# A searched instruction order and u on another DMA queue in an RWKV-6 and squared-ReLU kernel

## The chip, the cores and the metric

The kernel runs on one core of one Trainium2 chip. The metric is the device time of one execution in microseconds (us); lower is better. The engines of the core are TensorE (PE, with PEld for its weight loads), VectorE (DVE), ScalarE (ACT), GpSimd (POOL) and SyncE (SP). Each runs its own instructions strictly in the order in which the program gives them. SP only issues DMAs here.

## The reference

Two stages. The first is an RWKV-6 attention with B=4, H=8, S=768 tokens and head size D=48; r, k, v, w have the shape [B, H, S, D] and u has [H, D]:

```python
for t in range(S):
    cur = einsum('bhd,bhe->bhde', u[None] * kt, vt)
    y[:, :, t] = einsum('bhd,bhde->bhe', rt, state + cur)
    state = wt[:, :, :, None] * state + einsum('bhd,bhe->bhde', kt, vt)
```

Its output is laid out as x, [3072, 384], and goes through an MLP with w_in [384, 2048], w_out [2048, 384] and scalars s and b. The result is [3072, 384] in float32:

```python
h = x @ w_in
r = np.maximum(h, 0.0)
g = s * (r * r) + b
out = g @ w_out
```

## The kernel before

**The work.** The 3072 tokens are 24 chunks n of 128 tokens. Within a chunk the recurrence is done with matrix products, and a small state goes from a chunk to the next one of its batch. Two chunks make a token tile T of 256 tokens, and the MLP runs tile by tile (T = 0 to 11). Chunks 0 to 3 are "packed": they are loaded in pairs of 384 KB (load2, L316), the others by four loads of 192 KB (load, L308).

**The steps of a chunk**, by the names that the order uses: `load n.0` to `n.3` bring w, r, k and v. `ln` (ACT, L331 and L339) takes the log of w, `cum` (PE, L390 to L414) sums it over the chunk, `exp` and `exn` (ACT, L438, L456) and `inc` (DVE, L446) turn the sums into decay factors, `mul` (DVE, L465 and L472) multiplies r and k by them into the tile prd. `rkp` and `rku` (POOL, L344, L350) form r*k and then times u, `cd` (DVE, L367) sums that over a head, `yd` (POOL, L373) multiplies v by it. The transposed r and k (tile RK) come for n < 9 from TensorE (`tr`, L521) and a copy `tev` (L535 on ACT, L537 on DVE), and from n = 9 on from a DMA transpose on SP's queue, which is also called `tev` (dtrans, L558). `mt` (PE, L588 and L600; one step for two chunks) forms the products of k and r, `msk` (DVE, L612) masks them, `ymm`, `ydm`, `ymi` (PE) form y, `dmm` (PE), `sup` (DVE) and `st` (POOL) bring the state forward, `yev` (L741) writes y as x. x is transposed on TensorE for n < 20 (`xtr`, L787, with the copy `xev`) and by a DMA transpose from n = 20 on (dxtr, L568). `vb` casts v to bf16 on the engine that its label names.

**The steps of a tile.** `g1` T.0 to T.7 are 6 matmuls each (L841), `relu` follows on ACT (L854), `sq` squares on ACT (L864) or DVE (L866), `g2` T.0 to T.7 are 4 matmuls each (L884), `oev` scales and adds the bias on DVE (L895), and `store` writes on SP's queue (L913, L917). `li`, `lo` load the weights in pieces and `ci`, `co` cast them; `csred`, `csadd`, `cssplit`, `csspread`, `csevac` form the bias b * sum(w_out). `load_u` (L983) loads u as one row, `u_mm` (L987) spreads it over the partitions with two matmuls, and `u_ev` copies it out; rku needs it.

**What sets the order.** ORDER (from L42) is a list of all steps, written out as text. The program walks it, and each step issues its instructions on its engine, so the list fixes every engine's order, and SP's queue as well: loads, DMA transposes and stores go into one queue in list order. `+n` puts n independent warm-up matmuls on TensorE (L1263). A suffix `@A`, `@D` or `@P` writes ACT, DVE or POOL into the step's entry. A step acts on it only where its function asks for it, as `move` (packed yev, tev, xev, u_ev), `square`, `cast`, `csred` and `csadd` do:

```python
def relu(T, i):
    rh = mlp.tile([128, FPQ, TOK], BF16, name="rh", tag="rh", bufs=4)
    nc.scalar.activation(out=rh, in_=hs[T, i], func=AF.Relu)
...
    if pl.ops["sq", T, i]["eng"] == "ACT":
        nc.scalar.activation(out=g, in_=rh, func=AF.Square)
    else:
        nc.vector.tensor_tensor(out=g, in0=rh, in1=rh, op=ALU.mult)
```

The unpacked yev is written with nc.vector in the same way as relu with nc.scalar. Tiles live in rings of buffers (5 for w, 8 for r and k, 6 for v, 6 PSUM buffers for products, 2 for u_ps, o_ps and the warm-ups), and a step that takes a buffer waits until the last user of the one before is done.

Of the kernel before, what the change touches and what calls it, by code (L numbers as in the profile page):

```python
# [18 lines left out]
U_AT = 3.5  # L19
# [23 lines left out]
load0.0 load_u load0.1 load0.2 ln0 +6 u_mm cum0.0 cum1.0 cum1.1 exp0.0 exp0.1 load2.0 li0 load2.1  # L43
exp1.0 u_ev@A l20 l21 load0.3 rkp1 rku1 load2.2 mul0.0 mul0.1 +4 tr0 exp1.1 mul1.0 ln2 +4 cum2.0
rkp0 mul1.1 tr1 tev0@D exp2.0 cum3.0 cd1 tev1@A vb0@A exp2.1 vb1@A +3 mt0 rku0 li1 cum3.1 ci0@A rkp3
exp3.0 rkp2 mul2.0 load2.3 msk1.0 exp3.1 ci1@A li3 li2 msk0.0 lo0 msk1.1 +3 ymm0.0 msk0.1 cd0 dmm0
ymm0.1 mul2.1 sup0 yd0 yd1 vb3@A vb2@A rku3 st0 mul3.0 l23 sup1 load4.0 tr2 ymi0 ydm0 lo1 rku2
mul3.1 tr3 tev2@A yev0@A xtr0 yev1@D xtr1 xev0@D ci3@P cd3 tev3@A xev1@A ci2@A mt2 cd2 g10.0 msk2.0
yd2 g10.1 l22 yd3 relu0.0 co0@A li4 msk3.0 msk2.1 co1@P g10.2 ymm2.0 lo2 ln4 lo3 load5.0 dmm2 msk3.1
sup2 ymm2.1 st2 g10.3 csred0@D ydm2 cum4.0 sq0.0@A relu0.2 ci4@P relu0.1 ymi2 yev2@D g10.4 sq0.2@A  # L50
relu0.3 xtr2 sup3 csred1@D exp4.0 sq0.1@D small2 g10.5 co2@D g10.6 xev2@A lo4 yev3@A xtr3 csadd1@D
sq0.3@A relu0.4 csred2@D relu0.6 load4.1 g10.7 relu0.5 g20.4 xev3@A sq0.4@A co3@D ln5 csadd2@D
sq0.5@A g20.0 cum4.1 g20.5 g20.1 g11.0 g11.1 load4.3 load7.0 csred3@D relu0.7 co4@D sq0.6@A csadd3@D
cum5.0 g11.2 sq0.7@A load5.1 load4.2 l24 csred4@D small cum5.1 g20.6 load5.2 relu1.1 relu1.0 g20.2
relu1.2 exp4.1 csadd4@D cssplit sq1.0@A load5.3 g20.3 g11.3 mul4 g11.4 vb5@P exp5.0 g11.5 exp5.1
sq1.1@A sq1.2@A vb4@A relu1.3 relu1.4 rkp4 rkp5 g20.7 csspread g11.6 tr4 load8.0 load6.0 csevac mul5
rku4 l25 oev0.1 relu1.5 tev4@A tr5 tev5@D oev0.0 rku5 dmm4 load7.3 load6.1 sup4 load6.2 relu1.6
g11.7 g21.0 mt4 msk4.0 msk5.0 load6.3 load7.1 sq1.3@A sq1.4@A sq1.5@A sq1.6@A relu1.7 st1 g21.1
g21.4 g21.5 dmm5 ln6 load9.0 msk4.1 cd4 yd4 ymm4 cum6.1 msk5.1 cum6.0 ln7 cd5 sup5 ln8 st4 exp6.0
cum7.0 g21.2 sq1.7@A exp6.1 vb6@A g21.6 cum7.1 yev4 exp7.0 vb7@P st5 ymm5 g21.3 xtr4 exp7.1 cum8.0  # L60
yd5 l26 ln9 mul6 tr6 yev5 xev4@D st3 load7.2 exp8.0 xtr5 dmm6 mul7 cum9.0 g21.7 tr7 tev6@A inc8
xev5@A sup6 load10.0 load11.0 l28 dmm7 load8.3 load8.1 load11.3 load9.1 l27 sup7 exp9.0 g12.0 g12.1
tev7@A relu2.0 inc9 oev1.0 rkp6 mt6 rku6 rkp7 relu2.1 store0.0 load8.2 msk6.0 sq2.1@A g12.2 ln10
sq2.0@A g12.3 st7 cd6 exn9 exn8 relu2.3 relu2.2 sq2.3@A load9.2 store0.1 msk6.1 oev1.1 g12.4 msk7.0
sq2.2@A rku7 st6 yd6 msk7.1 g22.0 ymm6 g22.4 load9.3 g12.5 cd7 yev6 relu2.4 ymm7 g12.6 yd7 vb8@P
xtr6 cum10.0 g12.7 rkp9 l29 mul8 ln11 relu2.5 exp10.0 rkp8 relu2.6 xev6@D load10.1 yev7 g22.1 inc10
xtr7 sq2.6@A xev7@D cum11.0 dmm8 l210 g22.5 tr8 load10.3 g13.0 sup8 mul9 load11.1 tev8@D inc11
sq2.4@A load10.2 relu2.7 exn10 load11.2 g13.1 sq2.5@A tev9 rku9 load14.1 g22.2 g13.2 g22.6 vb11@P
relu3.0 vb10@A sq2.7@A exp11.0 g22.3 load13.0 rku8 load12.0 g13.3 cd9 relu3.2 exn11 vb9@A sq3.2@A
relu3.1 dmm9 sq3.1@A sq3.0@D g22.7 g13.4 load12.1 g13.5 mul10 oev2.0 sup9 relu3.3 cd8 sq3.3@A mul11  # L70
l211 rkp10 yd8 rkp11 st8 yd9 mt8 relu3.5 relu3.4 oev2.1 g23.4 msk9.0 g23.5 g23.0 load13.1 msk8.0
msk9.1 sq3.5@A dmm10 g13.6 ln12 msk8.1 ymm9 ln13 sq3.4@A rku10 relu3.6 ymm8 cum13.0 yev9 sup10
cum12.0 g23.1 exp12.0 load13.2 g13.7 yev8 xtr9 tev11 sq3.6@A exp13.0 inc13 xtr8 g23.6 dmm11 g23.2
xev8@A st9 rku11 rkp13 xev9@A relu3.7 g14.0 cd10 tev10 inc12 cd11 sup11 sq3.7@A relu4.0 load12.3
store1.0 g14.1 mt10 relu4.1 msk10.0 msk10.1 msk11.0 load14.0 l213 l212 load12.2 store1.1 load15.1
load13.3 load15.0 store2.0 load18.0 rku13 st10 yd10 st11 g14.2 g14.3 g14.4 g23.7 msk11.1 exn12 g14.5
yd11 ymm11 ymm10 exn13 sq4.0@A relu4.2 relu4.3 ln14 relu4.4 load14.2 load16.0 oev3.1 mul12 yev11
yev10 sq4.3@A g23.3 vb12@A sq4.1@A sq4.2@D g14.6 cum14.0 xtr10 relu4.5 mul13 load15.2 g24.0 xev10@D
tev12 tev13 sq4.4@D xtr11 exp14.0 relu4.6 g24.1 g14.7 dmm12 xev11@A g15.0 inc14 l214 sq4.6@A sq4.5@A
oev3.0 load17.0 g15.1 g15.2 ln15 rkp12 exn14 relu4.7 sq4.7@A cum15.0 relu5.1 g24.4 g24.2 inc15  # L80
relu5.0 sq5.1@D sup12 exp15.0 vb13@A g15.3 g24.5 exn15 cd13 store2.1 dmm13 mul14 relu5.3 sup13 rku12
rkp15 cd12 relu5.2 l215 rkp14 ln16 sq5.0@A g24.6 rku14 rku15 g24.3 g15.4 relu5.4 sq5.3@A g15.5
relu5.5 mul15 oev4.0 mt12 msk12.0 g24.7 msk12.1 load14.3 load15.3 tev15 load16.1 st12 msk13.0 oev4.1
ln17 sq5.2@A g15.6 yd12 cum16.0 load16.2 cum17.0 msk13.1 sq5.4@A yd13 exp16.0 g25.4 g25.5 vb15@A
g25.0 vb14@P inc16 l216 st13 rkp16 relu5.6 ln18 ymm13 sq5.6@A ymm12 inc17 cd14 g25.1 tev14 g15.7
yev12 yev13 xtr12 sq5.5@A exp17.0 xev12@A relu5.7 exn16 exn17 load17.1 dmm15 load16.3 load19.0 xtr13
dmm14 g25.6 cum18.0 xev13@D sq5.7@A sup15 g25.2 store3.1 store3.0 g16.0 g25.7 sup14 mt14 inc18 mul16
msk14.0 relu6.0 exp18.0 l218 st15 yd14 vb16@P sq6.0@A g25.3 cd15 yd15 g16.1 g16.2 g16.3 load17.2
msk15.0 relu6.1 relu6.2 relu6.3 msk14.1 msk15.1 g16.4 oev5.1 g16.5 rkp17 ymm14 sq6.1@A relu6.4 ln19
mul17 oev5.0 l217 load18.3 st14 tev16 load18.1 relu6.5 yev14 tev17 load17.3 ymm15 g26.4 g16.6  # L90
load18.2 store4.1 store4.0 rku17 g16.7 rku16 sq6.3@A sq6.2@A sq6.5@A load20.0 yev15 sq6.4@D load21.1
xtr14 cum19.0 dmm16 g26.0 load21.0 load19.1 xtr15 g26.1 xev14@D relu6.6 g26.2 xev15@D sup16 relu6.7
sq6.7@A exp19.0 g17.0 g17.1 cd17 relu7.0 load20.1 inc19 cd16 sq7.0@A vb17@P yd16 vb18@A load19.2
mt16 msk16.0 msk16.1 g26.5 sq6.6@A g17.2 msk17.0 st16 relu7.1 g26.6 dmm17 sup17 msk17.1 g17.3 ymm16
g26.7 yev16 oev6.1 rkp18 relu7.2 relu7.3 ymm17 g17.4 load20.2 yd17 st17 g26.3 xtr16 oev6.0 sq7.1@A
exn18 xev16@D yev17 g17.5 g17.6 load21.2 load19.3 ln20 exn19 rku18 mul18 g27.4 xtr17 sq7.2@A relu7.4
g27.0 g17.7 sq7.4@A relu7.5 relu7.6 ln21 sq7.5@D store5.0 xev17@D cum20.0 sq7.3@A rkp19 relu7.7 cd18
g18.0 mul19 l219 g18.1 vb19@P rku19 exp20.0 sq7.6@A load22.0 inc20 sq7.7@D cum21.0 g18.2 g27.5 g27.1
g27.6 exn20 relu8.0 tev18 g18.3 relu8.1 relu8.2 exp21.0 g27.2 dmm19 store5.1 sq8.2@A g27.3 g27.7
mul20 inc21 exn21 dmm18 relu8.3 sq8.0@D tev19 sq8.1@A cd19 mul21 g18.4 load23.0 g18.5 yd19 rkp20  # L100
g18.6 sup18 tev21 sup19 oev7.1 oev7.0 relu8.4 ln22 yd18 rkp21 mt18 sq8.3@A relu8.5 g28.0 st18
msk19.0 supn21 msk18.0 msk19.1 tev20 msk18.1 load20.3 rku20 g28.4 g18.7 load22.1 store6.1 relu8.6
sq8.5@A ln23 cum22.0 g28.1 rku21 inc22 ymm18 cd20 cum23.0 ymm19 sq8.4@A relu8.7 exp23.0 g28.5 supn20
yev18 yev19 inc23 load22.2 xtr18 g28.2 xtr19 exp22.0 mt20 load23.1 msk20.0 load23.2 cd21 msk20.1
msk21.0 g28.6 yd20 exn22 sq8.7@A xev18@A xev19@A mul22 exn23 supn22 sq8.6@A store6.0 g19.0 load21.3
msk21.1 vb20@A g19.1 rkp22 g28.3 g19.2 relu9.1 ymm20 g19.3 g28.7 yd21 vb21@P relu9.0 yev20 oev8.0
relu9.2 sq9.1@D g19.4 g19.5 sq9.0@A relu9.4 relu9.5 relu9.3 store7.1 sq9.4@A g19.6 g19.7 sq9.3@A
g29.4 tev22 rku22 sq9.2@A mul23 oev8.1 g29.0 ymm21 xev20 sq9.5@D relu9.6 tev23 relu9.7 sq9.7@A rkp23
load22.3 sq9.6@A yev21 cd22 st19 xev21 yd22 vb22@P load23.3 g29.1 g29.2 g29.5 g29.6 mt22 g29.7 g29.3
msk22.0 msk23.0 g110.0 msk22.1 g110.1 vb23@P ymm22 relu10.0 rku23 msk23.1 oev9.1 relu10.1 yev22  # L110
store8.1 store7.0 g110.2 cd23 supn23 yd23 sq10.0@D g110.3 g110.4 g110.5 ymm23 oev9.0 store8.0
relu10.2 sq10.2@D yev23 store9.1 relu10.5 sq10.1@A xev22 relu10.3 sq10.3@A relu10.4 sq10.5@A xev23
# [56 lines left out]
def kernel(  # L169
# [812 lines left out]
    def load_u():  # L982
        nc.sync.dma_start(out=u_row, in_=u.rearrange("h d -> (h d)").unsqueeze(0))  # L983
# [320 lines left out]
```

## Time and profile before

| | |
|---|---|
| median of 7 runs | 182.85 us (181.62 to 183.75) |
| profiled execution | 183.69 us |
| its span | 181.9 us |
| granted TensorE clock | 0.998 |
| DMA | 34.53 MB, mean 190 GB/s, 110065 of 115722 packets under 512 bytes |
| chain that ended last | PE 67%, ACT 8%, DMA 8%, SPq 6%, POOL 4%, DVE 4% |
| largest lines in it | o_ps L884 28%, h_ps L841 26% |

The span is cut into slices or windows; for each engine its busy time is given, for the DMA the mean busy share of the core's 16 DMA engines (packets overlap, so that it can exceed 1). The line of a wait names the waiting engine and line, what ended the wait, the total, the number of waits and the longest. SPq is the queue of SyncE.

### The profile page before, as it was taken

The page shows a single profiled execution, that of the slowest core. Times are in us where ns is not written, and L with a number is a line of the kernel's source. Part 1 is how long each engine was busy: PE and PEld are TensorE (multiplying, and loading weights), DVE is VectorE, ACT ScalarE, POOL GpSimd, SP SyncE. Part 2 cuts the span into 40 slices and gives each one's busy share as a digit, 9 for nine tenths or more (in the row PEclk, how much of TensorE's full clock was granted, in tenths as well). Part 3 has the DMA queues.
Part 4 walks back from the last instruction along what each step waited for, and adds up shares of the span by engine and source line. Part 5 has one row for each costly group of instructions (what it writes and reads, how often), then busy time and mean ns, then how long its engine had stood idle before and what let it go on. Part 6 is the DMA issues. An engine that isn't in the chain of part 4 may idle for free.

```text
span 181.9 us, 4873 instructions
## 1 busy us (share of the span) xinstructions
PE 173.6 (95%) x1879; PEld 132.7 (73%) x1880; DVE 138.9 (76%) x251; ACT 142.9 (79%) x281; POOL 104.8 (58%) x141
## 2 busy tenths in 40 slices
PE   7997799997999899999999999999999999999993
PEld 2364578785688777878877879788787797796872
DVE  7588889888999698688699789687789796660342
ACT  3649899999799799799998769679858869257750
POOL 3786982007989797991769449495378373520000
PEclk9999999999999999999999999999999999999999
DMA  5999999989999899989985996999859854722022
GB/s 150 313 312 345 381 311 243 242 167 224 183 180 207 185 197 208 201 205 220 215 178 105 205 219 115 219 214 226 168 113 213 180 137 96 205 72 67 0 86 87
DMA packets 115722, 34.53 MB, mean 190 GB/s; under 512 B 110065, under 2 KB 113906, under 8 KB 115698
## 3 DMA queue, kind: packets, MB, share of 16 engines
q1 hardware_dynamic: 115698, 34.22, 80.3%
q8 instruction: 14, 0.23, 0.6%
q14 instruction: 10, 0.08, 0.1%
HBM read 25.17 MB, written 4.72 MB: 164 GB/s over the span
## 4 chain that ended last, share of the span: by engine, by line
PE 67%; ACT 8%; DMA 8%; SPq 6%; POOL 4%; DVE 4%; issue 2%; DVEq 0%; POOLq 0%
PE o_ps L884 28%; PE h_ps L841 26%; DMA wi_st<-in_moe_w_in_dram 4%; SPq L308 4%; PE mt_ps L600 3%; ACT rh L854 2%; PE y_ps L659 2%; DMA rkt<-in_k_dram 2%; ACT gT L864 2%; PE y_ps L650 2%; ACT RK L535 1%; DMA u_row<-in_u_dram 1%; ACT E L438 1%; POOL rkp L344 1%; DVE prd L472 1%
## 5 line engine op out<-in xcount | busy, mean ns | idle before, releaser
L884 PE MATMUL o_ps<-w_out,gT 128*128 128x384 bf16 (+2 forms) x400 | 72.3, 320 | 0.0
L841 PE MATMUL h_ps<-xT,w_in 128*128 128x256 bf16 x576 | 72.1, 273 | 0.0
L854 ACT ACTIVATE rh<-h_ps 128x512 bf16<-128x512 f32 x96 | 54.5, 597 | 17.1 <-PE h_ps L841 16.6
L841 PEld LDWEIGHTS <-w_in 128*128 128x128 bf16 x576 | 60.0, 110 | 5.7 <-ACT w_in L964 0.2
L884 PEld LDWEIGHTS <-gT 128*128 128x128 bf16 x400 | 35.9, 97 | 18.0
L864 ACT ACTIVATE gT<-rh 128x512 bf16<-128x512 bf16 x77 | 47.0, 634 | 0.4
L612 DVE TENSOR_TENSOR mt_sb<-mt_ps,tri_strict 128x512 bf16<-128x512 f32 x40 | 25.5, 684 | 6.0 <-PE mt_ps L600 5.8
L350 POOL TENSOR_TENSOR rku<-rkp,u_bc 128x384 f32<-128x384 f32 x24 | 26.8, 1122 | 0.7 <-DVE cd L367 0.2
L373 POOL TENSOR_TENSOR yd<-vt,cd 128x384 bf16<-128x384 f32 x20 | 17.9, 897 | 12.0 <-DMA vt<-in_v_dram 6.4
L472 DVE TENSOR_TENSOR prd<-rkt,E 128x768 bf16<-128x768 f32 x20 | 21.3, 1066 | 3.0 <-ACT rh L854 1.5
L344 POOL TENSOR_TENSOR rkp<-rkt 128x384 f32<-128x384 f32 x20 | 20.5, 1028 | 5.3 <-DMA rkt<-in_k_dram 5.2
L438 ACT ACTIVATE E<-cums 128x388 f32<-128x388 f32 (+2 forms) x32 | 15.3, 495 | 8.4 <-POOL rkp L344 2.4
L895 DVE SCALAR_TENSOR_TENSOR o_sb<-o_ps,s_bc,bconst 128x384 f32<-128x384 f32 (+2 forms) x25 | 14.8, 595 | 5.7 <-PE o_ps L884 5.6
L966 POOL CAST vb<-vt 128x384 bf16<-128x384 f32 x11 | 5.5, 503 | 19.5 <-DMA vt<-in_v_dram 19.5
L866 DVE TENSOR_TENSOR gT<-rh 128x512 bf16<-128x512 bf16 x19 | 10.4, 558 | 7.5 <-ACT rh L854 7.5
L508 POOL TENSOR_TENSOR l<-E,par 128x8 f32<-128x8 f32 x20 | 7.9, 400 | 12.0 <-ACT E L438 7.4
L776 POOL TENSOR_TENSOR st<-stmp,l 128x384 bf16<-128x384 bf16 x16 | 14.0, 872 | 0.4 <-DVE stmp L767 0.4
L741 DVE TENSOR_TENSOR x_sb<-y_ps,yd 128x384 bf16<-128x384 f32 x20 | 10.7, 551 | 4.0 <-PE y_ps L659 3.9
L367 DVE TENSOR_REDUCE cd<-rku 128x8 f32<-128x384 f32 x24 | 13.0, 543 | 0.3 <-POOL rku L350 0.3
L767 DVE TENSOR_TENSOR stmp<-d_ps,st 128x384 bf16<-128x384 f32 x16 | 8.6, 551 | 1.8 <-PE d_ps L724 1.7
L1263 PE MATMUL warm_ps<-warm_sb 128*128 128x512 bf16 x19 | 7.2, 520 | 1.2 <-DVE warm_sb L1222 1.2
L465 DVE TENSOR_TENSOR prd<-pkt,E 128x384 bf16<-128x384 f32 x8 | 6.4, 816 | 2.7 <-ACT E L438 2.6
(103 smaller groups left out, 205.3 us busy)
## 6 DMA issues: line engine op xcount, KB each, us to landing
wt<-in_w_dram SPq DMA_DIRECT2D x20, 192.0 KB, 4.0
rkt<-in_r_dram SPq DMA_DIRECT2D x20, 192.0 KB, 3.6
vt<-in_v_dram SPq DMA_DIRECT2D x20, 192.0 KB, 3.7
rkt<-in_k_dram SPq DMA_DIRECT2D x20, 192.0 KB, 3.8
out_dram<-o_sb SPq DMA_DIRECT2D x19, 192.0 KB, 2.8
wi_st<-in_moe_w_in_dram SPq DMA_DIRECT2D x3, 768.0 KB, 8.0
wo_st<-in_moe_w_out_dram SPq DMA_DIRECT2D x3, 768.0 KB, 6.8
pkt<-in_w_dram SPq DMA_DIRECT2D x2, 384.0 KB, 4.5
```

What stands on the lines that cost most here:

```text
L344: nc.gpsimd.tensor_tensor(out=rkp, in0=c["r"], in1=c["k"], op=ALU.mult)
L350: nc.gpsimd.tensor_tensor(out=rku.rearrange("t h d -> t (h d)"), in0=c["rkp"].rearrange("t h d -> t (h d)"), in1=u_bc, op=ALU.mult,)
L373: nc.gpsimd.tensor_tensor(out=yd, in0=c["v"], in1=c["cd"].unsqueeze(2).to_broadcast([128, H, D]), op=ALU.mult,)
L438: nc.scalar.activation(out=c["E"][:, x, 0:w], in_=ps[:, 0:w], func=AF.Exp, scale=-1.0 if packed(n) and x else 1.0,)
L472: nc.vector.tensor_tensor(out=prd[:, :, :, 0:D], in0=c["rk"], in1=c["E"][:, :, 0:HD].rearrange("t x (h d) -> t x h d", h=H), op=ALU.mult,)
L612: nc.vector.tensor_tensor(out=c["mt"][:, sg], in0=c["mt_ps"][sg], in1=(masks[:, n % 2] if packed(n) else tri_strict) .unsqueeze(1) .to_bro ...
L776: nc.gpsimd.tensor_tensor(out=c["st_new"], in0=c["stmp"].rearrange("q p (g e) -> q p g e", g=2), in1=c["l2"].unsqueeze(3).to_broadcast([12 ...
L841: nc.tensor.matmul(ps[:, f, :], lhsT=w_in_sb[PIECE[ft]][:, kt, :].rearrange("p (m j) -> p j m", j=PIECES[PIECE[ft]])[:, ft - F0[PIECE[ft]] ...
L854: nc.scalar.activation(out=rh, in_=hs[T, i], func=AF.Relu)
L864: nc.scalar.activation(out=g, in_=rh, func=AF.Square)
L884: nc.tensor.matmul(os_[T, k][:, cols], lhsT=gT[T][:, ft, tt * 128 : (tt + 1) * 128], rhs=w_out_sb[PIECE[ft]][:, ft - F0[PIECE[ft]], cols], ...
L895: nc.vector.scalar_tensor_tensor(out=o_sb[:, cols], in0=os_.pop((T, k))[:, cols], scalar=s_bc, in1=bconst[:, cols], op0=ALU.mult, op1=ALU.add,
```

## The change

Two things. First, u: its row is allocated and its DMA issued at the very start, on ScalarE's queue, ahead of the load of ACT's function table; the step load_u goes, and u_mm stands later in the list. Second, ORDER is replaced as a whole by another one, with labels of its own.

```diff
@@ constants
-U_AT = 3.5
@@ ORDER: its beginning, and the stretch up to the DMA transposes for mt16
-load0.0 load_u load0.1 load0.2 ln0 +6 u_mm cum0.0 cum1.0 cum1.1 exp0.0 exp0.1 load2.0 li0 load2.1
-exp1.0 u_ev@A l20 l21 load0.3 rkp1 rku1 load2.2 mul0.0 mul0.1 +4 tr0 exp1.1 mul1.0 ln2 +4 cum2.0
...
-yev12 yev13 xtr12 sq5.5@A exp17.0 xev12@A relu5.7 exn16 exn17 load17.1 dmm15 load16.3 load19.0 xtr13
-dmm14 g25.6 cum18.0 xev13@D sq5.7@A sup15 g25.2 store3.1 store3.0 g16.0 g25.7 sup14 mt14 inc18 mul16
-msk14.0 relu6.0 exp18.0 l218 st15 yd14 vb16@P sq6.0@A g25.3 cd15 yd15 g16.1 g16.2 g16.3 load17.2
-msk15.0 relu6.1 relu6.2 relu6.3 msk14.1 msk15.1 g16.4 oev5.1 g16.5 rkp17 ymm14 sq6.1@A relu6.4 ln19
-mul17 oev5.0 l217 load18.3 st14 tev16 load18.1 relu6.5 yev14 tev17 load17.3 ymm15 g26.4 g16.6
...
++9 load0.0 load0.2 load0.1 ln0 load2.0 li1 load0.3 cum0.0 exp0.0 cum1.0 load2.2 rkp1 cum1.1 load2.1
+mul0.0 exp0.1 exp1.0 u_mm mul0.1 exp1.1 ln2 mul1.0 +1 tr0 u_ev@A mul1.1 li0 rku1 tev0@D +2 tr1 li2
...
+yev13@A sup14 cum17.0 load21.1 inc16 g24.6 inc17 rku17 exp16.0 g15.5 xtr12 l216 rkp16 load17.3 exn16
+oev4.0 cd17 yd14 xtr13 exp17.0 xev12@A sq5.2@D relu5.5@D load19.0 load23.0 xev13@A store4.0 g15.6
+g24.7 sq5.3@A mul16 g15.7 st15 relu5.6@A exn17 load19.3 mt14 sq5.5@A relu5.7@A msk14.0 yd15 g16.0
+g25.4 msk14.1 sq5.4@A msk15.0 g25.5 sq5.6@A rku16 load18.3 msk15.1 vb16@A g16.1 cum18.0 load22.1
+rku19 oev4.1 g16.2 relu6.1@A relu6.0@A ln19 rkp18 g25.0 load20.2 ymm14 sq5.7@A g16.3 load21.2 l217
+dmm16 yev14@A exp18.0 rkp23 sq6.1@D cd16 g16.4 relu6.2@A load21.0 inc18 load21.3 yd16 relu6.3@A
+load22.2 store3.0 st14 mul17 ln20 sq6.3@A rku18 g25.1 xtr14 g16.5 sq6.0@A ymm15 tev17 tev16 g25.6
...
@@ start of the kernel's body
+    u_row = work.tile([128, HD], FP32, name="u_row", tag="inc", bufs=2)[0:1]
+    nc.scalar.dma_start(out=u_row, in_=u.rearrange("h d -> (h d)").unsqueeze(0))
     nc.scalar.preload_act_table_set("natural_log_exp_and_others")
...
-    u_row = work.tile([128, HD], FP32, name="u_row", tag="inc", bufs=2)[0:1]
...
-    def load_u():
-        nc.sync.dma_start(out=u_row, in_=u.rearrange("h d -> (h d)").unsqueeze(0))
...
-    add("load_u", "SP", 0.5, load_u, (), [], [], U_AT, dma=0.1)
-    add("u_mm", "PE", 0.85, spread_u, (), ["load_u"], [("o", ["u_ev"])], 2.0, lat=0.2)
+    add("u_mm", "PE", 0.85, spread_u, (), [], [("o", ["u_ev"])], 2.0, lat=0.2)
```

The number of steps is the same but for load_u, and so is the work of each. What differs is their order, the engine of some copies, casts and squares, and the warm-up matmuls, of which there are 17 (+9, +1, +2, +3, +2) in place of 20 (+6, +4, +4, +3, +3 at the places of the old list). The new list labels 26 of the 96 relus @D and all the yevs @A or @D.

## The prediction

> **What bounds the kernel now.** I read the engine totals and the slices first, then the stages, then the waits of SP's queue and the chain around 40 us.
>
> ```profile
> span 181.9 us, 4873 instructions
> PE 173.6 (95%) x1879; PEld 132.7 (73%) x1880; DVE 138.9 (76%) x251; ACT 142.9 (79%) x281; POOL 104.8 (58%) x141
> ...
> DMA  5999999989999899989985996999859854722022
> ...
> q1 hardware_dynamic: 115698, 34.22, 80.3%
> ```
>
> TensorE is the bound on average. The profiled execution took 183.69 us, 1.79 more than its span and 0.84 more than the median of 182.85, so I add my changes to 183.69 and take 0.84 off at the end. The second thing to see is the DMA row: from 5 to 95 us it is as full as TensorE, and one queue, q1, carries nearly all of it. The stages (PE, PEld, DVE, ACT, POOL busy, granted clock, DMA share, GB/s) say the same:
>
> ```profile
> 10.00:20.00 10.00, 8.03 (x137) 4.94 (x137) 8.49 (x15) 6.86 (x13) 7.54 (x8) 1.00 1.06 344
> ...
> 30.00:40.00 10.00, 10.00 (x79) 7.54 (x77) 8.95 (x14) 9.70 (x22) 0.00 (x0) 1.00 0.79 187
> 40.00:50.00 10.00, 8.97 (x108) 6.26 (x107) 8.80 (x15) 8.59 (x18) 7.99 (x11) 1.00 1.11 208
> ...
> 100.00:120.00 20.00, 20.00 (x235) 15.99 (x233) 16.22 (x30) 15.85 (x33) 12.47 (x17) 1.00 0.92 192
> ```
>
> After 45 us TensorE is never idle, and it still sits at 10.00 of 10.00 while DMA runs at a share of about 1: transfers arrive just in time, and there is little to gain but much to lose in their order. The one place where a load shows on the path is load5.2 (k of chunk 5), which mul5 and tr5 wait for:
>
> ```profile
> 37.94 3.14 DMA rkt<-in_k_dram
> ...
> 41.20 0.97 DVE prd L472
> 42.17 0.05 issue
> 42.22 0.62 PE trps L521 x8
> ```
>
> SP's queue itself stops at the DMA transposes (L558), which must wait for prd, and everything issued behind them waits too:
>
> ```profile
> SPq L917 <- DVE o_sb L895: 14.5, 5, 7.1
> SPq L558 <- DVE prd L472: 13.4, 7, 3.2
> SPq L558 <- PE h_ps L841: 6.4, 5, 2.8
> ```
>
> **What the change costs, part by part.**
>
> *u on ScalarE's queue.* It takes one issue from SP (0.47 us in the chain of the first 25 us) and puts one of that kind at the head of ACT, before its table load; ACT's first work there waits for loaded data, so I cost it at nothing, at most 0.5 us if that cover is gone. u_mm (two matmuls, 1.61 us) leaves the place ahead of cum0.0, which began at 5.70 although ln0 had ended at 5.14 and a constant that it needs was ready at 5.2: at most 0.5 us earlier. Three warm matmuls fewer are 3 x 0.216 = 0.65 us of TensorE.
>
> [...]
>
> *Engines.* From the order that each engine gets: squares on ACT 77 to 79, tev on ACT 6 to 2, xev 10 to 8, casts of v from 13 ACT, 11 POOL to 14 ACT, 5 POOL, 5 DVE, some weight casts exchanged. At the shortest repeated durations of the trace (sq 0.52 ACT, 0.34 DVE; tev 0.91 and 0.60; xev 0.37 and 0.27; v cast 0.40 and 0.46; relu 0.48) the totals move from 134.2 to 134.4 us on ACT, 123.6 to 125.7 on DVE, 89.6 to 86.4 on POOL, 165.8 to 165.1 on PE. None of these is a bound. The 26 relu@D and 12 yev@A (chunks from 4) do nothing: relu calls ScalarE at L854 and the unpacked yev VectorE at L741 whatever the label says.
>
> *VectorE beside GpSimd.* If the new order keeps mul and POOL's products apart, it shortens the stretched ones:
>
> ```profile
> L472 DVE TENSOR_TENSOR prd<-rkt,E x20: 942/950/1751, 39.6 to 149.2; 128x768 bf16<-128x768 f32 x20
> ```
>
> The 20 took 21.3 us, 2.3 more than 20 x 0.95. VectorE is busy for 76%, so all of it lies beside TensorE's work; I cost it at nothing, -2.3 us at the outside. The median is near the minimum although POOL is busy most of that time.
>
> [...]
>
> *The ramp.* Following the new order through the same durations, g10.0 begins at 21.3 instead of 22.04 us, 0.7 earlier. The 1.3 us that TensorE lost before 45 us for load5.2 may go as well, and some 0.4 of smaller gaps: a gain of 1.1 us if load5.2 lands as before, 2.5 if all of it goes.
>
> *The order of transfers.* This decides. From chunk 9 on, the transposed r and k come from DMA transposes, which stand in the same SP queue as loads and stores; mt(n) needs them. I counted what the new order puts ahead of the last transpose that each pair needs. Loads before and after: mt8 32 to 37, mt10 38 to 45, mt12 48 to 56, mt14 53 to 63, mt16 59 to 76, mt18 71 to 79, mt20 72 to 80 (192 KB each; 8 packed loads ahead of all). Buffers for the early loads come free at least 7 us before they are wanted, so SP does issue them early. At mt16 the transposes and weights ahead are the same, the stores one more.
>
> In the profile the second transpose for mt16 (tev17) had landed at 116.53, and mt16 began at 117.88 us, unhindered. A 192 KB load in full stretches takes 0.98 us on average (best 0.90: six landed in 5.56 us from 120.35 on; worst 1.09), a store 0.55. Seventeen loads and a store more are 17 x 0.98 + 0.55 = 17.2 us of transfer ahead of it: 133.7 if no gap is filled. The gaps of before: the stage table's DMA shares up to 116.5 us sum to 109.4. Filled to a share of 1.0 that gives 7.1 us back (126.6); filled to 1.08, the mean of the full stretches (1.06, 1.11, 1.05, 1.10), it gives 15.2 back (118.5). I take the middle, 122.5, which is also what adding up the new queue's loads at 0.98 gives; at 0.90 that sum gives 116.5.
>
> Back to back (g1 and g2 0.65 us a step, mt 0.55, ymm 0.37) TensorE has 105.3 us of work ahead of mt16 in the old order, so 117.88 - 105.3 = 12.6 us had been lost by then. The new order has 104.1, and loses 10.6 if 0.7 of the ramp and the 1.3 of load5.2 are won: it would be there at 114.7, so it waits some 8 us, spread over mt10 to mt16. Behind mt16 lie 60.8 us of TensorE work (60.3 before). So the end stays where it was if mt16 begins at 117.88 - 0.5 = 117.4; it begins 0.3 after the landing, at 122.8: +5.4 us. What waits behind mt16 on TensorE are the matmuls of the MLP, since its queue is in order; ScalarE and VectorE starve with it. The ramp's gain disappears into this wait.
>
> **Sum.** 183.69 + 5.4 = 189.1 for a profiled execution, 188.3 for the median. Landing at 118.5 gives +1.4 (184.3), at 126.6 +9.5 (192.3).
>
> **Rivals.**
>
> *Faster: the loads are hidden.* If transfers keep the best rate and every gap is filled, the transposes land by 116.5 or earlier, TensorE waits little, and the ramp's 1.1 to 2.5 us stay: 180.4 to 181.8, say 181.2. For it: the full stretches reach 1.10, and 10.00 of 10.00 on TensorE held through all of them. Against: 0.90 held for six loads only, and from 48 to 67 us loads took 1.04 to 1.09.
>
> *Same: the labels.* The order was laid out as if 26 relus ran on VectorE; 26 x 0.478 = 12.4 us lie on ACT instead. Until tile 7 the excess never runs above 1.5 us, the rest falls where ACT has some 8 us to spare. If that 1.5 is paid and transfers are hidden, the ramp's 1.1 is eaten: about 183.2.
>
> *Worse: SP stalls on top.* Late mt means late buffers, so SP waits as it did at 95 to 100 us, where the DMA share fell to 0.48 (2.6 us lost). One more such stop and the drift of 2.2 us that landings showed from 46 to 65 us make 5.4 + 4.8: 193.1.
>
> **How the numbers follow.** Late transposes 0.52, worse 0.17, hidden and faster 0.22, labels 0.09, some of which ends above. What this kernel's measurement can tell from no change is about 0.5% (0.9 us). The forecast is the first case, 188.3; its own range is 184.3 to 192.3. For 8 in 10 the range reaches into the faster case, to 181.0, and to 192.8 above. Faster by over 0.5% 0.22, within 0.07, slower 0.71.
>
> **What would show it.** Right: TensorE idle at L600 with the DMA transposes (RK, L558) as the releaser from mt10 on, the most at mt16 around 115 to 123 us; DMA share at 1.0 or above without a dip until then; loads of chunks 18 to 23 landed long before their ln and mul. The ramp: g10.0 near 21.3. Wrong: TensorE busy 10.00 of 10.00 from 50 to 120 us, or its idle time put down to ACT's gT or rh; then the transfers were not the limit and the time falls to 181 to 183.

## The result and the profile after

The changed kernel takes 195.95 us (median of 12 runs, 194.18 to 198.31) where the kernel before takes 182.83 (31 runs): a ratio of 1.0701, 95% interval 1.067 to 1.0733. That is 13.1 us slower, in the direction of the forecast but above its range (181.0 to 192.8). Ratios are of undisturbed executions alone, while the profiles of the runs e2, e3, e6, e10 and e12 below come from disturbed ones, so that from these I read where things happen and take the gain or loss of a run from its ratio.

The page of the changed kernel: span, busy time of each engine, the row of the granted TensorE clock and that of the DMA engines.

```profile
span 194.0 us, 4877 instructions
PE 177.4 (91%) x1876; PEld 133.7 (69%) x1877; DVE 137.7 (71%) x257; ACT 142.3 (73%) x281; POOL 102.5 (53%) x135
...
PEclk9999589999999999999997999999999999999999
DMA  6999989999798998998998999999092422210113
```

DVE, ACT and POOL are busy for about as long as before (138.9, 142.9, 104.8). TensorE shows 3.8 us more busy time for less work: the clock row has a 5 in the fifth slice and a 7 in the 22nd, where the old row was all 9 (one digit is a 40th of the span, in tenths of the full clock). The DMA row is nearly full up to 135 us and then falls off; before, the same 34.5 MB were spread further.

What TensorE's matmuls waited for (engine, line, releaser: total, times, longest):

```profile
PE mt_ps L602 <- DMA RK<-prd: 4.3, 3, 2.3
PE xt_ps L789 <- ACT x_sb L537: 2.4, 1, 2.4
...
PE trps L523 <- DVE prd L474: 0.8, 1, 0.8
```

L602 is mt of the changed kernel (L600 before): it waits for the DMA transposes, which it never did before. The second line is new too, and was not in the prediction. The chain of waits between 82 and 106 us shows where the first one ends last (start, duration, what):

```profile
82.17 2.88 DMA RK<-prd
85.05 0.05 issue
85.09 0.40 PE mt_ps L602 x8
...
96.60 3.45 DMA RK<-prd
100.05 0.05 issue
100.10 0.62 PE mt_ps L602 x16
```

Was RK late because prd was, or because its transpose stood in the queue? The timelines of VectorE (first fence) and of SP's queue (second) answer it for mt12:

```profile
82.27 0.96 DVE L474 TENSOR_TENSOR prd<-rkt,E 128x768 bf16<-128x768 f32 x1 [0.70 <-ACT E L440]
...
89.44 0.96 DVE L474 TENSOR_TENSOR prd<-rkt,E 128x768 bf16<-128x768 f32 x1 [1.56 <-DMA rkt<-in_k_dram]
```

```profile
89.92 1.28 SPq L310 DMA_DIRECT2D vt<-in_v_dram  x2
91.25 0.73 SPq L310 DMA_DIRECT2D rkt<-in_r_dram  x1
92.03 1.93 SPq L310 DMA_DIRECT2D rkt<-in_k_dram  x2
94.05 0.76 SPq L310 DMA_DIRECT2D wt<-in_w_dram  x1
94.92 2.94 SPq L560 DMA_TRANSPOSE RK<-prd  x2
```

The prd of chunk 12 was ready at 83.23; its transpose is the second of the pair and was issued at 96.60, 13.4 us later. That of chunk 13, ready at 90.39, was issued at 94.92. In the kernel before the same two were issued 1.7 and 1.3 us after their prd (85.08 to 86.75, 87.21 to 88.53):

```profile
84.13 0.95 DVE L472 TENSOR_TENSOR prd<-rkt,E 128x768 bf16<-128x768 f32 x1
...
86.26 0.95 DVE L472 TENSOR_TENSOR prd<-rkt,E 128x768 bf16<-128x768 f32 x1
```

```profile
86.75 3.03 SPq L558 DMA_TRANSPOSE RK<-prd  x2
```

In the changed kernel, between 83.23 and 96.60, SP issued eleven loads, up to k of chunk 23, two store DMAs and the other transpose.

To place the loss I take each step's start less the TensorE work ahead of it in its own list (back-to-back durations, as in the prediction). This lateness, before and after: mt4 11.2 and 12.1; g13.0 (some 65 us) 12.0 and 14.8; mt12 12.4 and 22.5; g16.0 12.4 and 24.8; last matmuls 13.0 and 25.8. The last difference of 12.8, less 0.7 us of work that the new list saves, is the 12.1 us between the spans.

### The profile page after: what moved, and what is told of

The parts are those of the page before. It is cut to its first block, busy times and chain, and to the rows that moved or that the text cites. A ratio compares the mean times of both kernels' runs of the same rounds, so it can differ in the third digit from the quotient of the medians.

```text
span 194.0 us, 4877 instructions
## 1 busy us (share of the span) xinstructions
PE 177.4 (91%) x1876; PEld 133.7 (69%) x1877; DVE 137.7 (71%) x257; ACT 142.3 (73%) x281; POOL 102.5 (53%) x135
## 2 busy tenths in 40 slices
DMA packets 115721, 34.53 MB, mean 178 GB/s; under 512 B 110065, under 2 KB 113906, under 8 KB 115698
## 3 DMA queue, kind: packets, MB, share of 16 engines
q1 hardware_dynamic: 115696, 34.22, 76.3%
## 4 chain that ended last, share of the span: by engine, by line
PE 58%; ACT 14%; DMA 11%; SPq 6%; DVE 6%; issue 3%; ACTq 0%; DVEq 0%
PE h_ps L843 26%; PE o_ps L886 21%; ACT rh L856 5%; ACT gT L866 5%; DMA wi_st<-in_moe_w_in_dram 4%; SPq L318 3%; DMA RK<-prd 3%; DMA wt<-in_w_dram 3%; PE mt_ps L602 2%; DVE prd L474 2%; PE y_ps L661 2%; ACT E L440 1%; PE xt_ps L789 1%; PE y_ps L652 1%; SPq L915 1%
## 5 line engine op out<-in xcount | busy, mean ns | idle before, releaser
L843 PE MATMUL h_ps<-xT,w_in 128*128 128x256 bf16 x576 | 76.3, 281 | 1.0 <-ACT rh L856 0.5
L866 ACT ACTIVATE gT<-rh 128x512 bf16<-128x512 bf16 x79 | 48.5, 648 | 0.3
L352 POOL TENSOR_TENSOR rku<-rkp,u_bc 128x384 f32<-128x384 f32 x24 | 24.7, 1033 | 4.5 <-DVE cd L369 3.3
L346 POOL TENSOR_TENSOR rkp<-rkt 128x384 f32<-128x384 f32 x20 | 22.1, 1111 | 1.7 <-DMA rkt<-in_k_dram 1.7
L897 DVE SCALAR_TENSOR_TENSOR o_sb<-o_ps,s_bc,bconst 128x384 f32<-128x384 f32 (+2 forms) x25 | 14.8, 595 | 11.4 <-PE o_ps L886 10.4
L778 POOL TENSOR_TENSOR st<-stmp,l 128x384 bf16<-128x384 bf16 x16 | 18.2, 1144 | 0.5 <-DVE stmp L769 0.5
L868 DVE TENSOR_TENSOR gT<-rh 128x512 bf16<-128x512 bf16 x17 | 7.4, 441 | 11.0 <-ACT rh L856 11.0
L602 PE MATMUL mt_ps<-RK 48*128 48x128 bf16 x160 | 6.7, 218 | 5.1 <-DMA RK<-prd 4.3
L510 POOL TENSOR_TENSOR l<-E,par 128x8 f32<-128x8 f32 x20 | 5.1, 259 | 11.3 <-ACT E L440 11.3
L968 POOL CAST vb<-vt 128x384 bf16<-128x384 f32 x5 | 3.4, 685 | 12.8 <-DMA vt<-in_v_dram 12.8
L602 PEld LDWEIGHTS <-RK 48*128 48x128 bf16 x160 | 4.6, 94 | 8.1 <-DMA RK<-prd 5.4
```

The lines of the kernel that those rows point to most:

```text
L346: nc.gpsimd.tensor_tensor(out=rkp, in0=c["r"], in1=c["k"], op=ALU.mult)
L352: nc.gpsimd.tensor_tensor(out=rku.rearrange("t h d -> t (h d)"), in0=c["rkp"].rearrange("t h d -> t (h d)"), in1=u_bc, op=ALU.mult,)
L602: nc.tensor.matmul(ps[i][sg][:, p, :], lhsT=cb[m]["KT"][pr, p, :], rhs=cb[m]["RT"][pr, p, :], start=True, stop=True,)
L778: nc.gpsimd.tensor_tensor(out=c["st_new"], in0=c["stmp"].rearrange("q p (g e) -> q p g e", g=2), in1=c["l2"].unsqueeze(3).to_broadcast([12 ...
L843: nc.tensor.matmul(ps[:, f, :], lhsT=w_in_sb[PIECE[ft]][:, kt, :].rearrange("p (m j) -> p j m", j=PIECES[PIECE[ft]])[:, ft - F0[PIECE[ft]] ...
```

## The experiments

The theories: T, the new order puts loads ahead of transfers that are needed sooner, and TensorE waits for what is late; E, the engines' own new order is too tight; L, the labels that do nothing; C, a stop of TensorE costs more than itself, through the clock. All kernels are compared with runs of the kernel before on the same chip.

**e1, u alone.** The old list without load_u, u's DMA on ScalarE's queue, u_mm behind cum1.1:

```diff
-load0.0 load_u load0.1 load0.2 ln0 +6 u_mm cum0.0 cum1.0 cum1.1 exp0.0 exp0.1 load2.0 li0 load2.1
+load0.0 load0.1 load0.2 ln0 +6 cum0.0 cum1.0 cum1.1 u_mm exp0.0 exp0.1 load2.0 li0 load2.1
```

> The kernel before with only the first part of the change: u's DMA on ScalarE's queue at the start, u_mm behind the first sums (after cum1.1); all else in the old order. Every theory here has the loss in the new order, so 182.3 to 183.3 us, no measurable change. If the move of u itself is what costs, it shows as over 184.

Measured: 183.56 us, ratio 1.0052 (1.0004 to 1.0099). cum0.0 begins at 5.18 instead of 5.63, as costed, but u_mm now delays u_ev on ScalarE (9.08 instead of 8.10) and g10.0 begins at 23.16 instead of 22.04. By mt4 the delay is down to 0.4 us (44.61 and 44.24), since the wait for load5.2 swallows most of it. So u's move wins nothing and costs at most 1%, and the loss lies in the new order.

**e2, loads later.** The changed kernel; only load steps of chunks 8 to 23 move down the list, for example v of chunk 12:

```diff
-ln11 g12.1 yd6 sq2.0@A load12.3 g21.7 sup7 mt6 oev1.0
+exn8 relu2.2@A yev6@D relu2.4@A load12.3 load10.1 g12.5 yd7 load10.3
```

> The changed kernel with one thing altered: loads of chunks 8 to 23 are put later in the list, so that none stands more than 6 us of TensorE work ahead of its first reader. Loads ahead of the DMA transposes fall from 37, 45, 56, 63, 76 to 32, 38, 49, 57, 69 for mt8 to mt16 (before: 32, 38, 48, 53, 59); every compute engine keeps its order and its labels. Theory T (the transposes stand in SP's queue behind loads issued early): the waits at L602 for RK (4.3 us) and the slow clock behind the last of them (0.5 from 101 to 105 us) go, some 8 us less, 187 to 189 us. Theory E (the engines' new order and labels leave too little slack, the transposes are late because mul is late): 194 to 196 us, as the changed kernel.

Measured: ratio 1.0416 (1.0319 to 1.0512), some 191 us: between the two. What TensorE waited for:

```profile
PE xt_ps L789 <- ACT E L440: 2.7, 1, 2.7
PE xt_ps L789 <- ACT x_sb L537: 2.2, 1, 2.2
...
PE trps L523 <- DVE prd L474: 0.8, 1, 0.8
...
PE mt_ps L602 <- DMA RK<-prd: 0.5, 1, 0.5
```

Of the waits for RK 0.5 us is left of 4.3, and up to mt10 lateness stays level (14.6 at g13.0, 14.9 at mt10, where the changed kernel had 18.7). Then a new stop of 2.7 us opens before xtr10: its chain goes over VectorE (inc, oev, cd) back to a load of v that landed at 88.94. The clock falls to 0.5 behind it until 97 us. A cap on all loads alike put some that were needed soon too late. T was right about RK, but its 187 to 189 us were missed: my repair was too coarse.

**e3, the cast behind the copies.**

```diff
-li4 ci2@A mul3.0 ydm0 mul3.1 ymi0 rkp2 yev0@A sup1 lo3 yev1@A xtr0 tr3 load4.1 tev2@A
+li4 mul3.0 ydm0 mul3.1 ymi0 rkp2 yev0@A sup1 yev1@A xtr0 tr3 load4.1 tev2@A ci2@A lo3
```

> The changed kernel with the cast ci2 (and the load lo3 that waits for its buffer) moved behind tev2, so that yev0 and yev1 on ScalarE no longer stand behind a cast that waits for its weight piece (landed 16.87 us). The 2.4 us stop of TensorE before xtr0 and the half clock from 19 to 26 us should go: g11.0 some 4 to 5 us earlier. Theory T: what the transposes' landing sets swallows most of it, 193 to 195 us at the end. Theory A (the losses simply add up): 191 to 192 us.

Measured: ratio 1.0606 (1.0548 to 1.0665) where the changed kernel has 1.0701 (1.067 to 1.0733), 1.7 us less, where 4 to 5 us less had been costed for the ramp and T's range was 193 to 195 us at the end. In the profiled execution (198.56 us) the stop before xtr0 shrank from 2.44 to 1.23 us and the clock stayed at 1.00 up to 30 us; g11.0 came only 1.6 us earlier (30.55). A later w_out cast then held g20.1 for 1.4 us, and tr7 stood 1.8 us for prd (mul7 took 1.80 us there instead of 0.96, for a reason given behind the experiments), so that g12.0 was 3.4 us later than in the changed kernel. In this execution the gain was gone before 58 us.

**e4, warm matmuls in the stop.** 11 matmuls, ahead of xtr0, into a PSUM tile of their own:

```diff
-        for _ in range(n):
-            nc.tensor.matmul(
-                warm_ps, lhsT=...
+        ps = warm_ps
+        if n > 9:
+            ps = psP.tile([128, 2 * TOK], FP32, name="warm2_ps", tag="P")
+        for _ in range(n):
+            nc.tensor.matmul(
+                ps, lhsT=...
```

> The changed kernel with 11 more warm matmuls (2.4 us of TensorE work into a PSUM tile of their own that nothing reads) between ymi0 and xtr0, where TensorE stood still for 2.44 us. The stop stays as long, but TensorE is busy in it. Theory C (it is the stop that brings the granted clock to 0.5 from 19 to 26 us): clock 1.00 there and g11.0 about 3 us earlier than in the changed kernel; at the end 193 to 195 if the transposes decide, 192 to 193 if losses add up. If the clock falls for another reason (say total load), it stays at 0.5 and the time at 196.

The stretch of the ramp in windows of 2 us (PE, PEld, DVE, ACT, POOL busy, granted clock, DMA share, GB/s), first of the changed kernel, then of e4:

```profile
16.00:18.00 2.00, 0.36 (x6) 0.20 (x4) 1.05 (x3) 1.11 (x1) 2.00 (x3) 1.00 1.10 352
18.00:20.00 2.00, 1.20 (x14) 1.02 (x14) 0.56 (x2) 2.00 (x5) 1.34 (x2) 0.81 0.92 204
20.00:22.00 2.00, 1.54 (x36) 1.28 (x36) 2.00 (x5) 1.83 (x3) 0.44 (x1) 0.50 0.97 346
22.00:24.00 2.00, 2.00 (x11) 1.45 (x10) 2.00 (x5) 0.95 (x2) 2.00 (x4) 0.50 0.92 298
```

```profile
16.00:18.00 2.00, 1.95 (x13) 0.97 (x13) 1.13 (x3) 1.06 (x1) 2.00 (x3) 1.00 1.10 351
...
20.00:22.00 2.00, 1.59 (x42) 1.50 (x43) 2.00 (x6) 2.00 (x4) 0.57 (x1) 1.00 0.93 323
22.00:24.00 2.00, 2.00 (x26) 1.88 (x25) 2.00 (x4) 1.97 (x5) 1.98 (x4) 1.00 0.86 226
```

In 22 to 24 us TensorE is busy throughout in both, but a step of g1, 6 matmuls, takes 1.28 us in the one and 0.65 in the other. So C holds for this stop in this profile (e9 below adds four executions): with the array kept busy the half clock stayed away. g11.0 came 2.4 us earlier (29.70 for 32.10). The end did not: ratio 1.0786 (1.0738 to 1.0833), a little worse than the changed kernel and above all that had been expected. g20.1 now stood 2.9 us waiting for w_out, whose piece and cast came no earlier, and tr7 again stood 1.8 us for a mul7 of 1.80 us, so that g12.0 began at 55.86 instead of 53.96.

**e5 and e6, cheaper transfers** in the changed kernel and in the one before. The loads read contiguous rows, so they bring other tokens' values and the results are not those of the reference; the work behind them is the same:

```diff
-            out=dst, in_=src[bb, :, t0 : t0 + L, :].transpose([1, 0, 2])
+            out=dst,
+            in_=src[bb].rearrange("h s d -> (h s d)")[t0 * HD : (t0 + L) * HD]
+            .rearrange("(t h d) -> t h d", t=L, h=H),
```

> The changed kernel with cheaper transfers and nothing else altered: the 192 KB loads of chunks 4 to 23 read 128 contiguous rows of 1536 bytes instead of rows of 192 bytes (so they bring other tokens' values of the same tensor: the values are wrong, the work after them is the same). The packed loads, in rows of 384 bytes, moved 384 KB in 1.27 us, so I expect 0.65 us or less a load instead of 0.98. Theory T (the new order puts the transfers on the path: transposes, w_out pieces and w for ln come late): the waits for RK and for wt go; what stays is the stop before xtr0 with its slow clock, some 2 to 3 us, so 183 to 187 us. Theory E (the engines' order itself is too tight): 192 to 196 us.

> The kernel before with the same cheaper loads (values wrong in the same way), as the yardstick for the changed kernel with them. The 1.3 us wait for load5.2 goes, otherwise transfers were hidden: 181.0 to 182.5 us by theory T and by theory E.

Measured: e5 187.38 us, ratio 1.0273 (1.0235 to 1.0311); e6 ratio 0.997 (0.992 to 1.002). Packets fell from 115721 to 44041, and the queue's share of the DMA engines' time from 76.3% to 61.8%. Cheaper transfers win nothing clear of noise in the kernel before and 8.6 us in the changed one. This is the experiment that decides for T: no engine's order or label was touched. Its span is 185.1 us. What is left of TensorE's waits in e5:

```profile
PE xt_ps L791 <- ACT x_sb L539: 2.4, 1, 2.4
...
PE trps L525 <- DVE prd L476: 1.0, 1, 1.0
```

No RK, and lateness is 13.8 at mt4, 15.2 at mt12 and 16.8 at the last matmuls. Of the 3.8 us of lateness over the kernel before that remain at the end, 2.6 had been made by mt4 (46.38).

**e7, the labels obeyed.**

```diff
-        nc.scalar.activation(out=rh, in_=hs[T, i], func=AF.Relu)
+        if pl.ops["relu", T, i]["eng"] == "DVE":
+            nc.vector.tensor_scalar_max(rh, hs[T, i], 0.0)
+        else:
+            nc.scalar.activation(out=rh, in_=hs[T, i], func=AF.Relu)
```

> The changed kernel with its 26 labels relu@D obeyed: these relus run on VectorE. Theory L (the order was laid out for VectorE to do them, and ScalarE's extra 12.4 us make it late): 3 us or more faster than the changed kernel, 190 to 193 us. Theory T: ScalarE's lateness comes from waits for loads, most of these relus lie behind the last late transpose, so within 1 us of the changed kernel, 195 to 197.

Measured: 195.66 us, ratio 1.0734 (1.069 to 1.0778). ACT fell to 129.9 us busy, DVE rose to 154.1, and mt waited as before:

```profile
PE mt_ps L602 <- DMA RK<-prd: 4.0, 3, 2.3
```

L falls: 12 us taken off ScalarE change nothing.

**e8, the kernel before with early loads.** Loads of chunks 8 to 23 moved up to the changed kernel's distance from their first reader, all else in the old order.

> The kernel before with one thing altered: loads of chunks 8 to 23 stand as early in the list as the changed kernel has them in TensorE work ahead of their first reader, where buffers allow. Loads ahead of the transposes rise from 32, 38, 48, 53, 59 to 35, 44, 49, 55, 63 for mt8 to mt16. Theory T: the transposes for mt10 land some 6 us later than in the kernel before, where they had 3 to 4 us in hand, so TensorE stops there for 1 to 3 us: 184 to 187 us. Theory E: no change, 182.5 to 183.5.

Measured: 187.15 us, ratio 1.0234 (1.0163 to 1.0304). The size is T's, the place is not the one that I named: mt10 never stopped. TensorE stood still for 1.2 us from 50.9 on, before cum9.0, and for 1.5 from 53.2 on, before tr7, and the chain of the second stop is

```profile
49.92 3.61 DMA rkt<-in_k_dram
53.52 0.04 DVEq L472
53.56 0.04 issue
53.60 1.06 DVE prd L472
54.66 0.05 issue
54.71 0.62 PE trps L521 x8
```

The load in it is load7.2 (k of chunk 7): loads of chunks 8 to 11 had gone ahead of it in the queue. With the old engine order, early loads alone cost 2.3%.

**e9, cheaper transfers and warm matmuls together** (the edits of e4 and e5).

> The changed kernel with both the cheaper loads (contiguous rows of 1536 bytes, values of other tokens) and the 11 warm matmuls in the stop before xtr0. With cheap loads alone it took 187.4 us, 4.9 over the kernel before, all of it lost by 45 us. Theory C (the half clock from 19 to 26 us, set off by the stop, makes 3 us of that): 184 to 185 us. If the gain is given back as with the normal loads (there g20.1 then waited 2.9 us for w_out), it stays at 187.

Measured: 185.89 us, ratio 1.0156 (1.0102 to 1.0211), 1.5 us less than e5. The mean granted clock is 0.997 or more in all four executions, where it was 0.982 in all four of e5; g11.0 begins at 29.98 (31.98 in e5), and this time most of it is kept to the end: the last matmuls start at 180.07, not 181.80. So it was transfers that had taken back most of the gain of e4. It is a little above the 184 to 185 that C gave; by the ratio some 2.9 us over the kernel before remain (1.7 in the profiled spans), which I did not take apart. What E could be worth lies within them.

**e10, the transposes on ScalarE's queue.**

```diff
-        nc.sync.dma_start_transpose(
+        nc.scalar.dma_start_transpose(
```

> The changed kernel with its 15 transposes of prd and 4 of x issued on ScalarE's queue instead of SP's; order, loads and stores as they are. Theory T, in its form that the place in the one queue is what delays them: the waits at L602 for RK and the slow clock at 101 go, 188 to 191 us, unless ScalarE, which now waits in order for prd before each transpose and spends some 1.3 us on each, loses the same again (then 194 to 200, with PE waiting for rh and gT). If all 16 DMA engines being full is what delays them, whatever the queue, RK is as late as before: 195 to 197.

Measured: 203.88 us (199.67 to 205.54, 4 runs; no interval). The waits of TensorE between 60 and 130 us:

```profile
PE o_ps L886 <- ACT gT L866: 3.6, 2, 2.3
PE h_ps L843 <- ACT xT L537: 2.0, 2, 1.6
...
PE mt_ps L602 <- DMA RK<-prd: 0.3, 1, 0.3
```

The wait for RK falls from 4.3 to 0.3 us with the DMA engines as full as before (share 1.14 from 90 to 100 us, 1.08 in the changed kernel). The transposes of chunks 10, 11 and 12 are issued 3.4, 2.4 and 6.0 us after their prd, instead of 10.0, 9.1 and 13.4. So it was mostly the place in SP's queue that delayed them. It is not all: RK of chunk 12 landed at 98.54, just ahead of mt12 at 98.59, and the wait is short also because TensorE stood elsewhere first. ScalarE lost more than was won: the issue of one transpose took 1.25 to 2.17 us on its queue, and TensorE waited 5.6 us for the gT and xT that it makes.

**e11, one load moved in the kernel before** (load7.0 behind load5.2), and **e12**, the same with 7 warm matmuls in the ramp's gaps.

> The kernel before with load7.0 moved from its place ahead of load5.1 to behind load5.2. load5.2, for which mul5 and tr5 waited 1.3 us, lands one load (1 us) earlier. Theory T: 0.7 to 1.0 us less than before, a ratio of 0.995; if the wait passes on to something else, as with the cheaper loads in the kernel before, no change.

> The kernel before with load7.0 behind load5.2 (as in the run before this one, whose profile lost 1.7 us to a granted clock of 0.5 from 19 to 25 us although no stop of TensorE was longer than 0.72 us) and with 7 more warm matmuls in the three longest gaps of the first 22 us: 2 before the second half of ymm0, 3 before ydm0, 2 before mt2. Theory C (small gaps add up to the low clock): clock 1.00 from 19 to 25 us, g11.0 at 32 to 32.5, and with the wait for load5.2 gone 181.5 to 182.5, a ratio of 0.993 to 0.997. If what the ramp wins is taken back by later waits for transfers, as everywhere so far, no change.

Measured: ratios 1.0006 (0.997 to 1.0042) and 0.9988 (0.9958 to 1.0019), no change. The wait for load5.2 did go in e11. Its profiled execution lost about as much to the clock:

```profile
20.00:22.00 2.00, 1.54 (x38) 1.25 (x35) 1.62 (x4) 1.97 (x3) 2.00 (x3) 0.50 1.12 359
22.00:24.00 2.00, 2.00 (x14) 1.43 (x11) 2.00 (x4) 1.33 (x2) 2.00 (x4) 0.50 1.05 403
```

In e12 the clock stayed at 1.00 and mt4 began at 43.55 (before 44.24), but g12.0 at 54.22 (before 52.88): load7.2 landed 0.5 us later than before (51.62), and mul7, which waited for it, took 1.79 us instead of 0.96. No version was found that beats the kernel before.

## Why the prediction was right, and where it was wrong

*Right: the mechanism, not its size.* The order of transfers decides (e5, e8), in part through the transposes behind early loads (the queue's timeline, e10). I had TensorE waiting some 8 us for RK from mt10 to mt16; it waited 4.3, at mt10 and mt12 alone. That its whole loss from g13.0 to mt12, 7.7 us (22.5 less 14.8), comes near the 8 is luck: the rest is shorter stops, of 0.7 us before mt8 and 0.6 before g23.4 and below that. (The profile puts the stop before mt8 down to a square on ScalarE; its RK had landed at 71.24 and it began at 71.32, so that may be a wait for RK too.) The labels and u are worth what I gave them, nothing or up to some 1% lost; the shares of the engines were not tested alone.

*Wrong: the ramp and the stretch behind it.* This is the term of the sum that failed. It had lateness 2.0 us below before (10.6 for 12.6), since the ramp and load5.2 were to be won; it was 2.8 above at g13.0. That is 4.8 of the 6.7 us by which the spans' difference (12.1) exceeds the forecast's (5.4). g10.0 did begin earlier (21.55; forecast 21.3, before 22.04) and the wait for load5.2 did go, but by mt4 (44.69 for 44.24) nothing of it was left. I had followed back-to-back durations, which know nothing of when a weight piece lands. ScalarE's timeline shows the step that failed:

```profile
16.89 1.47 ACT L966 CAST w_in<-wi_st 128x1536 bf16<-128x1536 f32 x1 [1.36 <-DMA wi_st<-in_moe_w_in_dram]
18.27 0.85 ACT L537 CAST x_sb<-yp_ps 128x384 bf16<-128x384 f32 x2
```

The new list puts ci2 ahead of yev0 and yev1 on ScalarE. Its piece landed at 16.87, so the copies, and xtr0 behind them, waited, though TensorE had been done with the sums that they copy at 16.36. I had looked for such blocking only at SP and at ln, and costed the copies by engine, not by their neighbours. From 44 to 65 us transfers were late again: ln9 held ScalarE's queue for 2.43 us until w of chunk 9 landed at 51.64, behind that of chunk 10, and mul7, which needs load7.2 from behind both, began at 52.48 and let tr7 wait 0.8 us. (The landing of load7.2 isn't in the trace, and the profile names ln9, which mul7 does not read; that it was load7.2 is inferred from the order. In e8 the chain shows it.)

*Wrong: no price for the clock.* A stop had been costed at its own length. After the stop before xtr0 the clock was 0.5 for 6.8 us, which is up to 3.4 us of work and part of the 4.8 above, and after that before mt12 for 3.4 us, 1.7 us of work. The second is most of the 2.3 us between mt12 and g16.0, which with the 4.8, less the 0.4 by which 7.7 falls short of the forecast wait, make up the 6.7.

*Wrong: the binding place.* I let mt16 decide, with 17 loads ahead; it was mt12, whose transposes landed at 100.05. The transposes of mt16, forecast to land at 122.5 (118.5 to 126.6), landed at 128.95: the gaps were not filled (DMA share 0.81 from 70 to 80 us, where SP's issues of stores took up to 2.4 us). But TensorE was by then so late that mt16 at 129.04 did not wait for them. The rival with SP stalls on top (193.1) came nearest, and the range had stopped below it.

*Misread: VectorE beside GpSimd.* I noted that the median of mul is near its minimum although POOL is busy most of that time, as if that spoke against a price of the overlap. It does not. In the profiles of the kernel before and of the changed one, wherever a mul and a POOL instruction overlap by more than 0.2 us (16 and 22 pairs), the one that began second took at least 15% longer than the shortest of its line; in the kernel before, all 4 late mul (1.42 to 1.75 us instead of 0.95) had begun second, and POOL products that did so took up to 1.79 us instead of 1.00. mul7 and the rkp that goes with it begin almost together. In the changed kernel mul7 is first, in e4 it is second by 0.01 us and costs tr7 0.84 us (it took 1.80 us in e3 too):

```profile
52.48 0.96 DVE L474 TENSOR_TENSOR prd<-rkt,E 128x768 bf16<-128x768 f32 x1 [1.05 <-ACT logw_two L341]
...
52.58 1.73 POOL L346 TENSOR_TENSOR rkp<-rkt 128x384 f32<-128x384 f32 x1
```

```profile
53.54 0.99 POOL L346 TENSOR_TENSOR rkp<-rkt 128x384 f32<-128x384 f32 x1
...
53.55 1.80 DVE L474 TENSOR_TENSOR prd<-rkt,E 128x768 bf16<-128x768 f32 x1 [1.17 <-ACT E L440]
```

*Slips that change nothing.* The 0.3 us from landing to start in the forecast of mt16 was an estimate; mt12 began 0.05 us after its landing. The gaps filled to 1.08 give 16.4 us (1.08 x 116.5 less 109.4), not 15.2, which puts the early landing at 117.3 and the middle at 122.0. And TensorE was not "never idle" after 45 us: it stood 0.46 us before xtr7 at 62.57.

What the ramp wins was mostly taken back behind it, as the prediction said of its own gain: e4, e11 and e12 ended no faster, and e1's delay shrank in the same way. Part was kept in e3 (1.7 us) and, with cheap transfers, in e9 (1.5).

## What to carry to other kernels

Where one queue feeds everything and is full (here q1, 80.3% of the 16 DMA engines' span in the kernel before), its order is a schedule of its own (early loads alone cost 2.3% in e8): price a reordering by what stands ahead of each transfer that someone waits for, and for every in-order engine ask which instruction at its head waits for a transfer (ci2 held ScalarE for 1.36 us, ln9 for 2.43). A stop of TensorE near 2 us must be priced with the slow stretch that may follow it (6.8 and 3.4 us at half clock behind stops of 2.44 and 2.27 us). Of two products on VectorE and GpSimd that wait for the same load, put the one on the path first (mul7 took 0.96 us as the first, 1.80 as the second). And a gain upstream of a full queue is not a gain until the next late transfer has been looked up (in e4 g11.0 came 2.4 us earlier and the end did not).

## What the runs showed of the hardware

The half clock lasted 6.8 and 3.4 us in the changed kernel, behind stops of TensorE of 2.44 and 2.27 us. In e3 a stop of 1.8 us was followed by it, while stops of 1.8 and 2.9 us in e4 were not. In e11 the clock fell with no stop over 0.72 us, in a stretch (14 to 20 us) where TensorE was busy for 4.21 of 6 us; the kernel before, busy for 4.21 us there too, kept the full clock. The rows, e11 first:

```profile
14.00:20.00 6.00, 4.21 (x78) 2.78 (x76) 5.60 (x11) 4.72 (x10) 5.51 (x6) 0.92 1.08 376
```

```profile
14.00:20.00 6.00, 4.21 (x89) 2.42 (x78) 5.75 (x11) 4.93 (x10) 4.45 (x5) 1.00 1.05 364
```

So neither the length of a stop nor the busy share of such a stretch tells by itself when the clock falls; no run here shows what else decides.
